# A fused attention-and-MLP kernel: its opening reordered between the queues and engines, its last tile split 512 + 128

## The chip, the cores and the metric

The kernel runs on one core of a Trainium2 chip. The core has five engines with instruction streams of their own: TensorE (PE in the profile; its weight loads are shown as PEld), VectorE (DVE), ScalarE (ACT), GpSimd (POOL) and SyncE (SP), which here only starts transfers and waits. ScalarE starts some transfers too. Each stream is in order: an instruction that waits for a semaphore holds up everything behind it on its engine. The metric is the device time of one execution in microseconds (us), the median of the runs; lower is better.

## The reference, cut to what matters

```
def _layernorm(x): return (x - mean(x)) / sqrt(var(x) + 1e-5)

x  = A_x                      # [1, 2048, 640], bf16
xn = _layernorm(x)
return x + _A_ref(xn, A_wqkv, A_w_phi, A_wo) + _B_ref(xn, B_w1, B_w3, B_w2)

# _A_ref: q, k, v = xn @ wqkv, 32 heads of 20;  pq = q @ w_phi, pk = k @ w_phi
#   phi = [softmax(p), softmax(-p)];  kv = phi_k^T v;  z = sum(phi_k)
#   o = (phi_q @ kv) / (phi_q @ z + 1e-6);  return o @ wo
# _B_ref: (silu(xn @ w1) * (xn @ w3)) @ w2, inner width 1536
```

So the layer norm of the 2048 tokens comes first, and nothing can be multiplied before the first tokens are loaded, normalized and transposed.

## The kernel before

The 2048 tokens are 16 tiles of 128 (tile 0 to 15), each 128 x 640, with tokens on the partitions (x_tok). A projection needs the normalized tile transposed (xnT: features on partitions, five chunks of 128). Tiles 0 to 3 are transposed on TensorE (five transposes each into PSUM, then a copy to xnT); the later ones by transfers.

The kernel is written as a small planner. Each helper (mm, act, tt, dma and so on) records an operation with an engine, the regions that it reads and writes, and a guessed duration; all are issued from one line (L102, transfers L114). Generators (norms, transposes, attention, mlps, outs and others, L729 to L913) yield steps in their own order, and done counts hold one generator back until another has got far enough. The loop at L922 always takes the step that by the guesses can start first; the order in which steps are taken is then fixed as each engine's instruction order, and waits are put in from the recorded regions. So a changed guess or a changed condition can change the order on every engine, while the durations on the chip are what they are.

The opening, which most of the change touches:

- first_loads (L414) issues the loads. SP: tile 0's columns 0 to 319, tile 1, tile 2, the second half of wv (the weights of V, columns 320 to 639), tile 3, the first thirds of w1 and w3, w_phi, and later loads. ScalarE: tile 0's columns 320 to 639, then the first half of wv.
- consts (L434) sets constants; its Exp on a dummy tile is there so that ScalarE's function table is loaded early.
- norms (L729) orders the layer norm of tiles 0 to 3. For tiles 0, 2 and 3 VectorE takes statistics of each half (ln_half, BATCH_NORM_STATS2), joins them (BATCH_NORM_AGGREGATE) and adds eps; GpSimd raises to the power -0.5 (a TENSOR_TENSOR on one column). For tile 1 ScalarE sums the tile and its squares (act_sum), and VectorE (scalar_op, and act_rstd with the eps) and GpSimd finish. ln_apply then normalizes the tile in place, on VectorE for tiles 0 to 3; "apply(t)" below.
- transposes (L791) runs xn_transpose (L515) for tiles 0 to 3 and, after tile 0's, eight dummy matmuls (idle, L510). Tile 0's five transposes are copied in two parts: three chunks by ScalarE, two by VectorE. Tiles 1 to 3 are copied whole by the engine that is free first by the guesses (evac).
- attention (L811) starts with dummy matmuls (warm_up), then multiplies V of tiles 0 to 3 in single steps: five matmuls of 320 columns for the first half of wv, then five for the second; "V0" to "V3" below. v_store writes V from PSUM.
- After that come the first MLP blocks, the fold of w_phi into the key weights, keys, key-value sums, queries, and the output tiles.

The end: out_tile (L696) adds attention and MLP outputs of a tile in PSUM, 17 matmuls over the inner chunks. The last tile (t = 15) does so in two parts, columns 0 to 383 and 384 to 639: 17 matmuls, an add of the residual on VectorE, and a store from SP for each, so that the first part's add and store run beside the second part's matmuls.

Of the kernel before, what the change touches and what calls it, by code (L numbers as in the profile page):

```python
# [43 lines left out]
class _Program:  # L44
# [127 lines left out]
    def commit(self, ops):  # L172
        for o in ops:
            o.idx = len(self.ops)
            o.deps = self.find_deps(o)
            t = self.free[o.eng]
            for d in o.deps:
                t = max(t, d.end + (0.03 if d.eng == o.eng else 0.07))
            o.start = t
            if o.dma:  # L180
                self.free[o.eng] = t + 0.45
                if "T" == o.part:
                    self.free[o.eng] = t + (1.28 if o.cost < 5e5 else o.cost / 105e3)
                self.bus = max(self.bus, t + 0.5) + o.cost / (280e3 if o.part else 305e3)
                if o.part and o.cost > 5e5:
                    self.bus = max(self.bus, self.free[o.eng] + 1.0)
                o.end = self.bus + (1.5 if t < 1 else 1.6 if t < 3.5 or o.part and o.cost < 2e5 else 2.6)
            else:
                o.end = t + o.cost
                self.free[o.eng] = o.end  # L190
            self.ops.append(o)
            if o.eng == "POOL" and not o.dma:
                self.pool = o
            for g in o.reads:
                if isinstance(g, tuple):
# [54 lines left out]
def bass_parallel_sum__linear_kernel_hedgehog__glu_gated_swiglu__prompt_kernel(  # L250
# [11 lines left out]
    bf = DT.bfloat16  # L262
    LAG = 4.0
    QLEAD = 2
    IDLE1, IDLE2 = 11, 8
    f32 = DT.float32
    P = _Program(nc)

# [145 lines left out]
    def first_loads():  # L414
        def half_wv(eng, a):
            P.dma(eng, wv[:, :, a:a + 320], wqkv_t[:, :, 2 * D + a:2 * D + a + 320])

        P.dma("SP", x_tok[:, 0, 0:320], x_t[:, 0, 0:320])
        P.dma("ACT", x_tok[:, 0, 320:D], x_t[:, 0, 320:D])
        load_x(1, 2)  # L420
        load_x(2, 3)
        half_wv("ACT", 0)
        half_wv("SP", 320)
        load_x(3, 4)
        w13(0, 512)
        P.dma("SP", phi_s[:], phi_t)
        P.dma("SP", wqkT[:, DC:2 * DC, :], A_wqkv[:, D:2 * D], True)
        load_x(4, 8)
        load_x(8, 12)
        load_x(12, 16)  # L430
        P.dma("SP", wqkT[:, 0:DC, :], A_wqkv[:, 0:D], True)


    def consts():  # L434
        memset("DVE", t1[:, 2, :], 0.0)
        memset("DVE", warm[:], 0.0)
        act(warm[:], warm[:], ACT.Exp)
        memset("POOL", ident[:], 0.0)
        select(ident[:], 0, [[-1, 128]], 1, ALU.not_equal, 1.0)
        memset("POOL", GM[:], 1.0)  # L440
        select(GM[:], 0, [[128, DC], [-DH, H]], 1, ALU.is_ge, 0.0)
        select(GM[:], DH, [[-128, DC], [DH, H]], -1, ALU.is_gt, 0.0)
        memset("POOL", mhalf[:], -0.5)
# [51 lines left out]

    def ln_apply(t):
        o, m, s, z = x_tok[:, t, :], mv[:, t, 0:1], rstd[:, t, 0:1], rstd[:, t, 1:2]
        if t < 4 or P.free["DVE"] < P.free["ACT"] + 0.45:
            P.op("DVE", "tensor_scalar", [o], [o, m, s],
                 (o, o, m, s, ALU.add if t == 1 else ALU.subtract, ALU.mult),  # L500
                 cost=0.4)
        else:
            P.op("ACT", "activation", [o], [o, s, z], (o, o, ACT.Identity), dict(bias=z, scale=s),
                 cost=0.9)
# [9 lines left out]

    def xn_transpose(t, k):  # L515
        dst = xnT[:, :, t * 128:(t + 1) * 128]
        for j, a, b in ((0, 0, 3), (1, 3, DC)) if t == 0 else ((0, 0, DC),):
            o = PSb[:, (k + j) * 1024:(k + j) * 1024 + 128 * (b - a)].rearrange("p (c n) -> p c n", n=128)
            for dc in range(a, b):
                tr(o[:, dc - a, :], x_tok[:, t, 128 * dc:128 * dc + 128])  # L520
            if t == 0:
                copy(("ACT", "DVE")[j], dst[:, a:b, :], o, 2)
            else:
                evac(dst, o)
# [171 lines left out]
    def out_tile(t, k):  # L696
        b, ti = divmod(t, 4)
        if t + 2 < T:
            load_xres(t + 2)
        chunks = [(oT[:, i, t * 128:(t + 1) * 128], wo_s, i) for i in range(DC)]  # L700
        chunks += [(hT[b][:, i, ti * 128:(ti + 1) * 128], w2_s, i) for i in range(FC)]
        if t == T - 1:
            for q, lo, hi in ((0, 0, 384), (1, 384, D)):
                for n, (l, w, i) in enumerate(chunks):
                    mm(bank(k + q, hi - lo), l, w[:, i, lo:hi], n == 0, n == len(chunks) - 1)
                r = xres[:, t % 4, lo:hi]
                tt("DVE", r, bank(k + q, hi - lo), r, ALU.add)
                finish.append(P.dma("SP", out_t[:, t, lo:hi], r))
            return
        for n, (l, w, i) in enumerate(chunks):  # L710
            for q in range(2):
                mm(bank(k + q, 320), l, w[:, i, 320 * q:320 * q + 320], n == 0, n == len(chunks) - 1)
        r = xres[:, t % 4, :].rearrange("p (b c) -> p b c", c=320)
        tt("DVE", r, bank2(k, 320), r, ALU.add)
        finish.append(P.dma("SP", out_t[:, t, :], xres[:, t % 4, :]))
# [8 lines left out]
                       default=0.0)  # L724
        return min((k for k in range(0, 8, n) if k // 2 not in held), key=free_at)

    done = dict.fromkeys(("w", "ln", "t", "f", "k", "n", "kv", "v", "u", "qp", "qn", "qd", "q", "o", "h"), 0)

    def norms():  # L729
        yield lambda: (first_loads(), consts())  # L730
# [3 lines left out]
        yield lambda: act_sum(1, ACT.Square, mv[:, 1, 1:2], mv[:, 1, 0:1])  # L734
        yield lambda: ln_apply(0)
        done["ln"] = 1
        yield lambda: act_rstd(1)
        yield lambda: ln_half(2, 0)
        while done["t"] < 1:
            yield None  # L740
        yield lambda: ln_apply(1)
        done["ln"] = 2
        yield lambda: ln_half(2, 1)
        yield lambda: ln_rstd(2, 1)
        yield lambda: ln_half(3, 0)
        yield lambda: ln_apply(2)
        done["ln"] = 3
# [37 lines left out]
    def transposed(t):  # L785
        while done["ln"] <= t:
            yield None
        yield lambda: xn_transpose(t, banks(1 if t else 2))
        done["t"] = t + 1

    def transposes():  # L791
        for t in range(4):
            yield from transposed(t)
            if t == 0:
                yield lambda: idle(IDLE2, 128)
# [15 lines left out]
    def attention():  # L811
# [4 lines left out]
        for t in range(4):  # L816
# [4 lines left out]
            for q in range(2):  # L821
                for i in range(DC):
                    yield lambda t=t, q=q, i=i, k=k: v_part(t, q, i, k)
            yield lambda t=t, k=k: v_store(t, k)
            held.clear()
        while done["f"] < 1:
# [194 lines left out]
```

## Time and profile before

| | us |
|---|---|
| median of 3 runs | 269.75 (269.71 to 269.94) |
| the profiled execution's own time | 269.72 |
| its span, first to last instruction | 268.0 |
| TensorE busy | 263.9 (98% of the span) |
| VectorE busy | 171.0 (64%) |
| GpSimd busy | 102.9 (38%) |
| ScalarE busy | 99.5 (37%) |

Times in the profile count from the start of the span; 1.72 us of the profiled execution's time lie outside it. A timeline line reads: start, length, engine, line, operation, output and input tiles, shape, count of merged instructions, and in brackets the idle time before it with what ended it. Matmuls are pipelined: the printed end of one lies behind the start of the next, so rates are taken from starts. "SPq" and "ACTq" are the transfers that SyncE and ScalarE start. Small tiles share names: t is the dummy tile and scratch t1, PS is PSUM, x_tok a token tile, bst and mv statistics, rstd the factor 1/sqrt(var + eps).

### The profile page before, as it was taken

What the parts mean: (1) busy time and instruction counts of PE and PEld (TensorE: products, weight loads), DVE (VectorE), ACT (ScalarE), POOL (GpSimd) and SP (SyncE); (2) the same over time, 40 slices, a digit from 0 to 9 for tenths busy, and PEclk for the clock granted to TensorE, in tenths of its full rate; (3) what the DMA queues carried; (4) which work ended last, traced back from release to release, by engine and by line L of the source; (5) the groups of instructions that cost most, each with busy time, mean ns of one, the idle gap of its engine ahead of it and who ended that gap; (6) DMA issues with size and microseconds to landing.
All of it is one profiled execution on the core that took longest, in us unless ns stands there. A gap on an engine that the chain in (4) does not pass through costs nothing.

```text
span 268.0 us, 4821 instructions
## 1 busy us (share of the span) xinstructions
PE 263.9 (98%) x1962; PEld 161.2 (60%) x1962; DVE 171.0 (64%) x292; ACT 99.5 (37%) x193; POOL 102.9 (38%) x143
## 2 busy tenths in 40 slices
PE   8999999999999999999999999999999999999996
PEld 4656677776745545555555455544577777777774
DVE  4559899998886878888888887888512121212112
ACT  5557979988324443344442344322100000000000
POOL 3316748999995364444444444420000000000000
PEclk9999999999999999999999999999999999999999
DMA  7997695900093444554444444214212213131301
GB/s 217 288 322 152 137 230 109 314 6 2 3 331 67 78 78 81 100 100 93 78 91 92 78 82 78 43 39 78 49 51 73 75 53 97 51 98 49 93 31 49
DMA packets 63510, 27.73 MB, mean 103 GB/s; under 512 B 49792, under 2 KB 63488, under 8 KB 63488
## 3 DMA queue, kind: packets, MB, share of 16 engines
q1 hardware_dynamic: 62688, 26.94, 41.9%
q10 hardware_dynamic: 800, 0.49, 0.7%
q8 instruction: 15, 0.25, 0.4%
q14 instruction: 7, 0.06, 0.1%
HBM read 12.81 MB, written 2.62 MB: 58 GB/s over the span
## 4 chain that ended last, share of the span: by engine, by line
PE 96%; DMA 1%; ACT 1%; DVE 0%; POOL 0%; issue 0%; SPq 0%
PE PS L102 96%; DMA x_tok<-in_A_x_dram 1%; ACT t L102 1%; POOL rstd L102 0%; DVE x_tok L102 0%; DVE xres L102 0%; SPq L114 0%; DVE rstd L102 0%; DVE mv L102 0%
## 5 line engine op out<-in xcount | busy, mean ns | idle before, releaser
L102 PE MATMUL PS<-xnT,w_s 128*128 128x512 bf16 x480 | 107.5, 379 | 0.0
L102 PEld LDWEIGHTS PS<-xnT,w_s 128*128 128x128 bf16 x480 | 45.8, 98 | 51.3 <-ACT Wkp L102 0.2
L102 PE MATMUL PS<-w_s,hT 128*128 128x320 bf16 (+2 forms) x384 | 54.9, 299 | 0.0
L102 DVE TENSOR_TENSOR xres<-PS,xres 128x640 bf16<-128x640 f32 (+2 forms) x17 | 13.4, 785 | 60.0 <-PE PS L102 60.0
L102 ACT ACTIVATE th<-PS 128x512 f32<-128x512 f32 x48 | 28.8, 600 | 49.1 <-PE PS L102 49.1
L102 PEld LDWEIGHTS PS<-w_s,hT 128*128 128x128 bf16 x384 | 37.6, 98 | 14.6
L102 DVE SCALAR_TENSOR_TENSOR t<-th,PS 128x512 bf16<-128x512 f32 x48 | 32.4, 675 | 21.2 <-ACT th L102 21.2
L102 POOL TENSOR_TENSOR ekt<-ekt,rS 128x640 bf16<-128x640 bf16 x32 | 39.5, 1265 | 0.6 <-DVE rS L102 0.6
L102 ACT ACTIVATE eq<-PS 128x600 bf16<-128x600 f32 (+1 forms) x72 | 24.7, 411 | 29.7 <-PE PS L102 29.6
L102 DVE SCALAR_TENSOR_TENSOR hT<-t,PS 128x512 bf16<-128x512 bf16 x48 | 33.0, 687 | 1.7
L102 PE MATMUL PS<-wv,xnT 128*128 128x320 bf16 x160 | 24.7, 299 | 0.1
L102 PE MATMUL PS<-wo_s,oT 128*128 128x320 bf16 (+2 forms) x160 | 24.5, 299 | 0.0
L102 PE MATMUL PS<-Wqp,xnT 128*128 128x512 bf16 (+1 forms) x160 | 24.1, 299 | 0.0
L102 PE MATMUL PS<-Wkp,xnT 128*128 128x320 bf16 x160 | 23.9, 299 | 0.0
L102 ACT ACTIVATE ekt<-PS 128x640 bf16<-128x640 f32 x32 | 22.3, 703 | 3.8 <-PE PS L102 3.3
L102 POOL TENSOR_TENSOR eq<-eq,rq 128x600 bf16<-128x600 bf16 (+1 forms) x32 | 22.6, 728 | 1.3
L102 DVE TENSOR_REDUCE S<-ekt 128x64 f32<-128x1280 bf16 x16 | 23.0, 1438 | 0.0
L102 POOL TENSOR_TENSOR rq<-rq,Sq 128x32 f32<-128x32 f32 x16 | 4.0, 252 | 48.8 <-DVE rq L102 48.8
L102 POOL TENSOR_TENSOR half<-eq 128x660 f32<-128x660 bf16 x15 | 20.4, 1358 | 3.6 <-ACT eq L102 3.6
L102 PEld LDWEIGHTS PS<-wo_s,oT 128*128 128x128 bf16 x160 | 15.7, 98 | 6.3
L102 PEld LDWEIGHTS PS<-wv,xnT 128*128 128x128 bf16 x160 | 15.3, 98 | 6.5 <-ACT xnT L102 0.5
L102 PEld LDWEIGHTS PS<-Wqp,xnT 128*128 128x128 bf16 x160 | 12.8, 97 | 10.5
(55 smaller groups left out, 182.9 us busy)
## 6 DMA issues: line engine op xcount, KB each, us to landing
w_s<-in_B_w_dram SPq DMA_DIRECT2D x6, 640.0 KB, 6.2
xres<-in_A_x_dram SPq DMA_DIRECT2D x16, 160.0 KB, 2.4
out_dram<-xres SPq DMA_DIRECT2D x15, 160.0 KB, 1.8
x_tok<-in_A_x_dram SPq DMA_DIRECT2D x3, 640.0 KB, 6.4
w_s<-in_B_w_dram SPq DMA_DIRECT2D x1, 1920.0 KB, 8.0
wo_s<-in_A_wo_dram SPq DMA_DIRECT2D x1, 800.0 KB, 8.2
x_tok<-in_A_x_dram SPq DMA_DIRECT2D x3, 160.0 KB, 3.9
wv<-in_A_wqkv_dram ACTq DMA_DIRECT2D x1, 400.0 KB, 4.4
```

Source lines behind the costliest of these rows:

```text
L102: o = _Op(eng, lambda: m(*args, **kw), r, w, cost)
```

## The change

Every edit is in the opening or in the last output tile, but for the planner's guesses, from which the whole order is made.

- The load of tile 2 moves from SP to ScalarE's queue, behind the dummy Exp (which moves ahead of it, with its memsets). The first half of wv moves from ScalarE to SP, into the place where tile 2's load was.
- Tile 2 is normalized by GpSimd (tensor_scalar, 128 x 640) instead of VectorE.
- In norms, tile 2's first statistics come before tile 1's eps, and its second before apply(1); tile 3's first statistics wait until tile 1's transposes are placed.
- Tile 1's transposes are placed only after five V matmuls of tile 0 (the count v0).
- The transposes of tiles 1 and 2 are copied in two parts by ScalarE and VectorE, as tile 0's were.
- Five dummy matmuls instead of eight after tile 0's transposes.
- The last tile is split into columns 0 to 511 and 512 to 639; the second part's store is started by ScalarE.
- The planner's guess of when a transfer lands changes for transfers not started by SP.

```diff
-                self.bus = max(self.bus, t + 0.5) + o.cost / (280e3 if o.part else 305e3)
+                self.bus = max(self.bus, t + 0.5 if o.eng == "SP" else 0.0) + o.cost / (280e3 if o.part else 305e3)
...
+                o.end = max(o.end, t + 2.2)
...
-    IDLE1, IDLE2 = 11, 8
+    IDLE1, IDLE2 = 11, 5
...
+        memset("DVE", t1[:, 2, :], 0.0)
+        memset("DVE", warm[:], 0.0)
         P.dma("SP", x_tok[:, 0, 0:320], x_t[:, 0, 0:320])
         P.dma("ACT", x_tok[:, 0, 320:D], x_t[:, 0, 320:D])
         load_x(1, 2)
-        load_x(2, 3)
-        half_wv("ACT", 0)
+        P.op("ACT", "activation", [warm[:]], [warm[:]], (warm[:], warm[:], ACT.Exp), {}, cost=1.4)
+        P.dma("ACT", x_tok[:, 2, :], x_t[:, 2, :])
+        half_wv("SP", 0)
         half_wv("SP", 320)
         load_x(3, 4)
...
     def consts():
-        memset("DVE", t1[:, 2, :], 0.0)
-        memset("DVE", warm[:], 0.0)
-        act(warm[:], warm[:], ACT.Exp)
...
-        if t < 4 or P.free["DVE"] < P.free["ACT"] + 0.45:
+        if t == 2:
+            P.op("POOL", "tensor_scalar", [o], [o, m, s], (o, o, m, s, ALU.subtract, ALU.mult), cost=0.9)
+        elif t < 4 or P.free["DVE"] < P.free["ACT"] + 0.45:
...
-        for j, a, b in ((0, 0, 3), (1, 3, DC)) if t == 0 else ((0, 0, DC),):
+        for j, a, b in ((0, 0, 3), (1, 3, DC)) if t < 3 else ((0, 0, DC),):
...
-            if t == 0:
+            if t < 3:
                 copy(("ACT", "DVE")[j], dst[:, a:b, :], o, 2)
...
-            for q, lo, hi in ((0, 0, 384), (1, 384, D)):
+            for q, lo, hi in ((0, 0, 512), (1, 512, D)):
...
-                finish.append(P.dma("SP", out_t[:, t, lo:hi], r))
+                finish.append(P.dma(("SP", "ACT")[q], out_t[:, t, lo:hi], r))
...
         done["ln"] = 1
+        yield lambda: ln_half(2, 0)
         yield lambda: act_rstd(1)
-        yield lambda: ln_half(2, 0)
         while done["t"] < 1:
             yield None
+        yield lambda: ln_half(2, 1)
         yield lambda: ln_apply(1)
         done["ln"] = 2
-        yield lambda: ln_half(2, 1)
         yield lambda: ln_rstd(2, 1)
+        while done["t"] < 2:
+            yield None
         yield lambda: ln_half(3, 0)
         yield lambda: ln_apply(2)
...
-        yield lambda: xn_transpose(t, banks(1 if t else 2))
+        yield lambda: xn_transpose(t, banks(1 if t > 2 else 2))
...
         for t in range(4):
+            while t == 1 and done["v0"] < DC:
+                yield None
             yield from transposed(t)
...
                     yield lambda t=t, q=q, i=i, k=k: v_part(t, q, i, k)
+                    done["v0"] += 1
```

More of the change, by code (lines that the diff above doesn't have):

```diff
@@ L725, in banks @@
         return min((k for k in range(0, 8, n) if k // 2 not in held), key=free_at)
-    done = dict.fromkeys(("w", "ln", "t", "f", "k", "n", "kv", "v", "u", "qp", "qn", "qd", "q", "o", "h"), 0)
+    done = dict.fromkeys(("w", "ln", "t", "f", "k", "n", "kv", "v", "u", "qp", "qn", "qd", "q", "o", "h", "v0"), 0)
     def norms():
```

## The prediction, made before the changed kernel was run

> **What bounds the kernel now.** I read the span first, then the chain of waits, then the timeline of the opening and of the last tile, then the landings of the first loads.
>
> ```profile
> span 268.0 us, 4821 instructions
> 6.02 0.17 DVE rstd L102
> ...
> 6.85 0.46 DVE x_tok L102
> 7.35 5.00 PE PS L102 x43
> ...
> 19.95 245.56 PE PS L102 x1826
> ```
>
> These pieces of the chain read start, length, what. From 7.35 us it is TensorE to the end of the last matmul; the part from 19.95 on is one unbroken piece of 1826. Work of the middle cannot be hidden better, it can only start earlier. So the edits can gain in two places only: gaps of TensorE before about 14 us, and what follows the last matmul. Ahead of 7.35 stands tile 1's normalization: from its eps instruction (6.02) to its transposes it is 1.33 us.
>
> ```profile
> 6.66 0.45 PE L102 MATMUL PS<-wv,xnT 128*128 128x320 bf16 x2
> 7.35 0.45 PE L102 MATMUL PS<-ident,x_tok 128*128 128x128 bf16 x5 [0.25 <-DVE x_tok L102]
> 7.64 1.79 PE L102 MATMUL PS<-wv,xnT 128*128 128x320 bf16 x12
> 9.29 0.45 PE L102 MATMUL PS<-ident,x_tok 128*128 128x128 bf16 x5
> 10.54 0.66 PEld L102 LDWEIGHTS PS<-wv,xnT 128*128 128x128 bf16 x6 [0.31 <-ACT xnT L102]
> 12.39 1.20 PEld L102 LDWEIGHTS PS<-wv,xnT 128*128 128x128 bf16 x10 [0.38 <-DVE xnT L102]
> 13.77 0.59 PE L102 MATMUL PS<-xnT,w_s 128*128 128x512 bf16 x2
> ```
>
> Printed ends overlap the next start, so I take rates from starts: twelve V matmuls from 7.64 to 9.29, 0.137 us each; five transposes from 7.35 to 7.64, 0.058 each. V of tiles 0 to 3 plus the transposes of tiles 1 to 3 need 40 x 0.137 + 15 x 0.058 = 6.35 us, but lie between 6.66 and 13.77, which is 7.11. So 0.76 us of gaps is all that reordering can win here: about 0.42 before 7.35 (6.66 + 2 x 0.137 = 6.93), the rest mainly where V2 waits at 10.54 for ScalarE's copy and V3 at 12.39 for VectorE's.
>
> **The change, part by part.** *Start of tile 0.* Its loads, statistics and transposes keep their order, so V0 still starts at 6.66: the 0.49 us copy below starts at 6.11. The three dummy matmuls left out lie in that wait: nothing, unless TensorE's clock fell in a longer wait; after the old gap of 0.42 us its rate was the full one above.
>
> ```profile
> 6.09 0.48 DVE L102 BATCH_NORM_STATS2 bst<-x_tok 128x6 f32<-128x320 bf16 x1
> 6.11 0.49 ACT L102 ACTIVATE xnT<-PS 128x384 bf16<-128x384 bf16 x1
> 6.49 0.27 DVE L102 COPY xnT<-PS 128x256 bf16<-128x256 bf16 x1
> 7.21 0.49 DVE L102 BATCH_NORM_STATS2 bst<-x_tok 128x6 f32<-128x320 bf16 x1
> 7.73 0.21 DVE L102 BATCH_NORM_AGGREGATE mv<-bst 128x2 f32<-128x12 f32 x1
> 7.84 0.70 ACT L102 ACTIVATE xnT<-PS 128x640 bf16<-128x640 bf16 x1 [1.24 <-PE PS L102]
> 8.15 0.49 DVE L102 BATCH_NORM_STATS2 bst<-x_tok 128x6 f32<-128x320 bf16 x1
> 8.21 0.55 POOL L102 TENSOR_TENSOR rstd<-rstd,mhalf 128x1 f32<-128x1 f32 x1 [1.39 <-DVE rstd L102]
> 9.15 0.49 DVE L102 BATCH_NORM_STATS2 bst<-x_tok 128x6 f32<-128x320 bf16 x1
> ```
>
> *Loads.* Tile 2's load leaves SP's third place; the first half of wv takes it. On ScalarE's queue the load stands behind the table load and the Exp:
>
> ```profile
> 0.79 1.34 SPq L114 DMA_DIRECT2D x_tok<-in_A_x_dram  x3
> 1.22 0.46 ACTq L114 DMA_DIRECT2D wv<-in_A_wqkv_dram  x1
> 1.71 1.28 ACT L102 ACT_TABLE_LOAD   x1 [1.71 <-PEq L1006]
> 2.17 0.43 SPq L114 DMA_DIRECT2D wv<-in_A_wqkv_dram  x1
> 3.01 0.21 ACT L102 ACTIVATE warm<-warm 128x8 f32<-128x8 f32 x1
> ```
>
> It is issued at about 1.22 + 1.28 + 0.21 + 0.05 = 2.76, a microsecond later than before (third of the three SP issues, about 1.70). When it lands decides the case. Landings, from DMA views of short windows (last number: us from issue), and the queues' traffic from 3.6 to 4.0 us:
>
> ```profile
> x_tok<-in_A_x_dram SPq DMA_DIRECT2D x1, 160.0 KB, 2.8
> wv<-in_A_wqkv_dram ACTq DMA_DIRECT2D x1, 400.0 KB, 4.4
> x_tok<-in_A_x_dram SPq DMA_DIRECT2D x1, 160.0 KB, 3.9
> wv<-in_A_wqkv_dram SPq DMA_DIRECT2D x1, 400.0 KB, 5.5
> ...
> q10 hardware_dynamic: 201, 0.13, 106.9%
> q1 hardware_dynamic: 3, 0.00, 1.1%
> ```
>
> Tile 1 landed at 1.24 + 2.8 = 4.0, the first wv half (ScalarE, q10) at 1.22 + 4.4 = 5.6, tile 2 (SP, q1) at 1.70 + 3.9 = 5.6, the second wv half at 2.17 + 5.5 = 7.65. While tile 2's load stood on q1, q10 moved 201 packets and q1 three: it got through only as the wv half ended. In the new order that half follows tile 1 on SP and still ends in front; if tile 2 then goes ahead of the second half, the same bytes have moved by the same time and it lands by about 5.6 again. I take 5.6; the other bound is 8.1 (a rival). The Trainium skill, page "DMA: Bandwidth & Descriptors", section "Queues, rings and completion order", says that a DMA engine takes turns between the queues' rings packet by packet. By that rule the load waits for one packet and 5.6 is an upper bound; 201 against 3 shows that the turns were not fine ones.
>
> *Tile 1.* VectorE's first statistics of tile 2 now stand ahead of tile 1's eps. They start at 5.6, as tile 2 lands; the eps follows 0.4 later, at 6.0, as before, since neighbours overlap by 0.08 (6.09 + 0.48 against 6.49). ScalarE's sums of tile 1 start earlier, because its load no longer shares with wv, but the eps is held by VectorE's order: no gain. While GpSimd raises to the power, VectorE copies (0.27) and does tile 2's second statistics (0.48), so apply(1) starts at 6.85 to 6.95 and the transposes at 7.35 to 7.45. Now the gap ahead of them holds five V matmuls instead of two: 6.66 + 5 x 0.137 = 7.34. After the transposes (7.64) come five V matmuls instead of eight; they need the second wv half, 7.65, so V0 ends at 8.38 where it was 7.64 + 8 x 0.137 = 8.74: 0.36 gained.
>
> *Tile 2.* Its second statistics no longer stand behind apply(1), so the aggregate comes at 7.21 instead of 7.73 and the power at 7.69 instead of 8.21, ending 8.24. GpSimd's apply follows at 8.30. Its price has no row:
>
> ```profile
> L102 POOL TENSOR_TENSOR ekt<-ekt,rS 128x640 bf16<-128x640 bf16 x32 | 39.5, 1265 | 0.6 <-DVE rS L102 0.6
> L102 POOL MEMSET GM<- 128x160 bf16 x1 | 0.2, 231 | 0.0
> ```
>
> It is below the two-input 1.27 us and not below VectorE's own 0.46 (6.85 in the chain). Four times the 160-column memset is 0.92; I take 0.95. The transposes are ready at 9.30, against 9.29 before. The Trainium skill, "GPSIMD Engine Reference", section "Engine selection", calls one-input work there roughly line-rate, an estimate of 640 / 1.2 GHz (the clock in its table) = 0.53 us plus dispatch; by that the sum would not change, since V1 covers it. V1 runs 8.38 to 10.02 with these five transposes inside. The copies are shared: ScalarE takes 0.49 instead of 0.70 and waits for three transposes instead of five (2 x 0.058), so V2 follows the transposes by 10.54 - 9.29 - 0.32 = 0.93 and starts at 10.23. That is 0.31 gained (at 1.27 us for the apply V2 starts at 10.55: nothing gained here).
>
> *Tile 3.* Its first statistics started at 8.15 and its second at 9.15, with VectorE's apply(2) between them. Now the second follow at 8.15 + 0.41 = 8.56, so everything behind them, to the transposes, is 0.59 earlier and falls into V2, and V3 does not wait as it did at 12.39. V2 ends at 10.23 + 1.37 + 0.29 = 11.89, the single copy (up to 0.70) is done by then, and V3 ends at 13.26 instead of 13.77. The opening gains **0.51 us**.
>
> *Last tile.* 34 matmuls over the same columns: by the 128- and 320-column rates time is linear in columns, so TensorE loses nothing.
>
> ```profile
> 263.68 0.56 DVE L102 TENSOR_TENSOR xres<-PS,xres 128x384 bf16<-128x384 f32 x1 [1.94 <-PE PS L102]
> 265.54 0.42 DVE L102 TENSOR_TENSOR xres<-PS,xres 128x256 bf16<-128x256 f32 x1 [1.30 <-PE PS L102]
> ...
> out_dram<-xres SPq DMA_DIRECT2D x1, 96.0 KB, 1.6
> ...
> out_dram<-xres SPq DMA_DIRECT2D x1, 64.0 KB, 1.5
> ```
>
> The add shrinks by 0.14 per 128 columns: 0.28 for 128, 0.70 for 512. The 512 add runs in the 17 x 0.058 = 0.99 us of the last part. The last store is half as long, but moves rows of 256 bytes and is issued by ScalarE: I put 1.5 again; the two rows, 0.1 apart for 32 KB, give 1.4 below, and 0.2 more than the nearest row, for the queue that no row shows storing, gives 1.7 above. The tail gains 0.14 (from 0.24 to a loss of 0.06).
>
> **Sum.** The profiled execution took 269.72 (0.03 below the median of 269.75): 269.72 - 0.51 - 0.14 = 269.07, call it **269.1**.
>
> **Rivals.**
> 1. *Slower: the loads are served in order of issue across both queues.* Tile 2 then follows both wv halves and lands about where tile 3's load, next to it in the issue order, landed before: 2.65 + 5.5 = 8.1.
>
> ```profile
> 2.65 0.52 SPq L114 DMA_DIRECT2D x_tok<-in_A_x_dram  x1
> x_tok<-in_A_x_dram SPq DMA_DIRECT2D x1, 160.0 KB, 5.5
> ```
>
> VectorE stands at its first statistics; behind them on that engine wait tile 1's eps, the copy that V0's fourth matmul reads, and apply(1). All shift by 8.1 - 5.6 = 2.5, so 271.6. For it: 201 packets against 3. Against: at 4.0 only the wv half, issued before tile 2, was in flight, and all of it may have counted as one turn. It decides from a landing at about 6.25, where the 0.65 gained is gone.
> 2. *Half the gain.* GpSimd's apply takes 1.27, or tile 2 lands near 6.0: V2 starts where it did, 0.2 around V3 and the tail remain: 269.72 - 0.2 - 0.14 = 269.4. For it: no row has this operation on GpSimd. Against: V1 leaves 0.4 us between the transposes' place and its end.
> 3. *The gain does not reach the end*, or the planner's new order differs: times after 14 us are fixed by loads, or it puts V0's second half ahead of tile 1's transposes and TensorE stands for the 7.65 landing. The tail alone remains: 269.72 - 0.14 = 269.6. Against: nothing after 19.95 waits now.
>
> **How the numbers follow.** Forecast 0.60, rival 1 0.16, rival 2 0.15, rival 3 0.09. The forecast's own range is 268.7 (all 0.76 and 0.24) to 269.3 (V0's 0.36 and 0.06); to leave out no more than 2 in 10 the range goes to 269.9, with most of rival 1 outside. No change means within 0.2%, about 0.54 us, which is what a measurement of this kernel can tell: 269.21 to 270.29. Faster: 0.56 of the forecast and 0.02 of rival 2, 0.58. Same: 0.04 + 0.13 + 0.08 = 0.25. Slower: 0.16 + 0.01 = 0.17.
>
> **What would show it.** In the new timeline: five V matmuls from 6.66, transposes at 7.35 to 7.45, V1 from about 8.4, V2 about 10.2, first 512-column matmul at 13.2 to 13.3; GpSimd's 640-column instruction near 8.3 with 0.9 us. VectorE idle before tile 2's first statistics, released by the x_tok load, would be rival 1. The last add should last 0.28. I am wrong if the chain of waits still shows VectorE, GpSimd or a load after 7.4, or if TensorE's unbroken piece begins much earlier and the span is the same.

## The result, and the profile after

| | before | after |
|---|---|---|
| median of 6 runs each, us | 269.76 (269.56 to 269.94) | 270.85 (270.58 to 271.40) |
| ratio to before, with its 95% interval | 1 | 1.0045 (1.0035 to 1.0055) |
| the profiled execution's own time and span | 269.72, 268.0 | 270.58, 268.8 |
| GpSimd busy | 102.9 | 105.4 |

The change makes the kernel slower by 0.45%, some 1.1 us. The forecast was 269.1, and 270.85 lies above the whole range (268.7 to 269.9). The profiled execution is the fastest of the six, so its trace shows 0.86 of the 1.1. The page of the changed kernel begins:

```profile
span 268.8 us, 4797 instructions
```

Its chain of waits (start, length, what) has, where before TensorE's unbroken work began at 7.35:

```profile
7.62 0.56 POOL rstd L102
...
8.28 2.54 POOL x_tok L102
...
11.79 3.17 PE PS L102 x25
```

GpSimd's one instruction on tile 2 holds the chain until 10.87. The timeline of the same kernel shows it together with a second, earlier wait:

```profile
6.63 0.85 PE L102 MATMUL PS<-wv,xnT 128*128 128x320 bf16 x5 [0.19 <-ACT xnT L102]
8.13 0.31 PE L102 MATMUL PS<-wv,xnT 128*128 128x320 bf16 x1 [0.65 <-DMA wv<-in_A_wqkv_dram]
8.28 0.44 PE L102 MATMUL PS<-ident,x_tok 128*128 128x128 bf16 x5
8.28 2.53 POOL L102 TENSOR_SCALAR x_tok<-x_tok,mv,rstd 128x640 bf16<-128x640 bf16 x1
9.75 0.57 PE L102 MATMUL PS<-wv,xnT 128*128 128x320 bf16 x3
10.87 0.45 PE L102 MATMUL PS<-ident,x_tok 128*128 128x128 bf16 x5 [0.55 <-POOL x_tok L102]
15.01 1.24 PE L102 MATMUL PS<-xnT,w_s 128*128 128x512 bf16 x5
```

First, the planner put not five but six V matmuls ahead of tile 1's transposes, and the sixth reads the second half of wv. TensorE stood from about 6.63 + 5 x 0.137 = 7.32 to 8.13 for that load, with tile 1's transposes, whose input VectorE had finished at about 7.25, queued behind it. Second, GpSimd's instruction took 2.53 us, so tile 2's transposes, ready to go at 9.75 + 3 x 0.137 = 10.16, started at 10.87. These two waits are 0.81 + 0.71 = 1.5 us, where V and the transposes had 0.76 us of gaps in all before. The first 512-column matmul is printed at 15.01 (before 13.77). Some records of matmuls are missing in this trace, so I trust the last add's start more: 266.56 against 265.54, 1.02 later.

The loads' issues, again from the timeline:

```profile
1.23 1.28 ACT L102 ACT_TABLE_LOAD   x1 [1.23 <-PEq L1014]
1.30 0.39 ACTq L114 DMA_DIRECT2D x_tok<-in_A_x_dram  x1
2.52 0.21 ACT L102 ACTIVATE warm<-warm 128x8 f32<-128x8 f32 x1
```

Their landings, from DMA views of short windows (last number: us from issue to landing), tile 1, tile 2 and the two halves of wv:

```profile
x_tok<-in_A_x_dram SPq DMA_DIRECT2D x1, 160.0 KB, 2.6
x_tok<-in_A_x_dram ACTq DMA_DIRECT2D x1, 160.0 KB, 2.8
...
wv<-in_A_wqkv_dram SPq DMA_DIRECT2D x1, 400.0 KB, 4.4
...
wv<-in_A_wqkv_dram SPq DMA_DIRECT2D x1, 400.0 KB, 5.9
```

Tile 2's load is behind the Exp in ScalarE's stream, but it was issued at 1.30, while the table load ran and 1.2 us before the Exp. It landed at 1.30 + 2.8 = 4.1, beside tile 1 (3.9); the halves of wv, issued at 1.71 and 2.18, came at 6.1 and 8.1. The tail, from the timeline:

```profile
266.56 0.29 DVE L102 TENSOR_TENSOR xres<-PS,xres 128x128 bf16<-128x128 f32 x1 [0.26 <-PE PS L102]
266.88 0.35 ACTq L114 DMA_DIRECT2D out_dram<-xres  x1
```

and the last store's landing, from the DMA view:

```profile
out_dram<-xres ACTq DMA_DIRECT2D x1, 32.0 KB, 1.5
```

From the last add's start to the end of the span it is 268.8 - 266.56 = 2.24, before 268.0 - 265.54 = 2.46: 0.22 gained. With 1.02 lost ahead of it that is the span's 0.8. The chain has GpSimd at 8.28, which is the prediction's own sign of being wrong (VectorE, GpSimd or a load after 7.4).

### The profile page after: what moved, and what is told of

The parts are those of the page before. It is cut to its first block, busy times and chain, and to the rows that moved or that the text cites. A ratio compares the mean times of both kernels' runs of the same rounds, so it can differ in the third digit from the quotient of the medians.

```text
span 268.8 us, 4797 instructions
## 1 busy us (share of the span) xinstructions
PE 261.7 (97%) x1939; PEld 159.8 (59%) x1959; DVE 170.9 (64%) x293; ACT 99.0 (37%) x193; POOL 105.4 (39%) x144
## 4 chain that ended last, share of the span: by engine, by line
PE 95%; POOL 1%; DVE 1%; DMA 1%; issue 1%; ACT 0%
PE PS L102 95%; POOL x_tok L102 1%; DMA x_tok<-in_A_x_dram 1%; DVE bst L102 1%; POOL rstd L102 0%; DVE x_tok L102 0%; ACT xnT L102 0%; DVE mv L102 0%; DVE rstd L102 0%; DVE xres L102 0%; DVE xnT L102 0%
## 5 line engine op out<-in xcount | busy, mean ns | idle before, releaser
L102 PE MATMUL PS<-xnT,w_s 128*128 128x512 bf16 x464 | 105.7, 379 | 1.0 <-ACT Wkp L102 0.2
L102 PE MATMUL PS<-Wqp,xnT 128*128 128x128 bf16 (+1 forms) x157 | 23.5, 297 | 0.2
L102 PEld LDWEIGHTS PS<-Wkp,xnT 128*128 128x128 bf16 x160 | 15.5, 98 | 6.0
```

What stands on the lines that cost most here:

```text
L102: o = _Op(eng, lambda: m(*args, **kw), r, w, cost)
```

## The experiments

Medians stand beside the runs of the kernel before on the same chip (269.62 to 269.75 in the different groups); ratios are to those.

### Each wait taken away alone, and both

Tile 2 normalized by VectorE again, everything else as changed:

```diff
-        if t == 2:
-            P.op("POOL", "tensor_scalar", [o], [o, m, s], (o, o, m, s, ALU.subtract, ALU.mult), cost=0.9)
-        elif t < 4 or P.free["DVE"] < P.free["ACT"] + 0.45:
+        if t < 4 or P.free["DVE"] < P.free["ACT"] + 0.45:
```

> The changed kernel with tile 2 normalized by VectorE again; nothing else is edited. Theory A (the loss is GpSimd's normalization, 2.53 us where 0.95 was expected): tile 2's transposes come at about 9.9 instead of 10.87, the first MLP matmul at 14.1 to 14.2 instead of 15.01, the time falls by about 0.85 to 270.0. Theory B (the loss is the later landing of the second wv half and TensorE standing for it at 7.3 to 8.1, with one V matmul of tile 0 in front of tile 1's transposes): that wait stays whole, and the time falls by 0.3 at most, 270.55 or more.

V0's second half held behind tile 1's transposes, with GpSimd's apply left in (a second condition keeps the later fold of w_phi where it was):

```diff
     def fold_k():
+        while done["v0"] < 8 * DC:
+            yield None
...
             for q in range(2):
+                while t == 0 and q == 1 and done["t"] < 2:
+                    yield None
                 for i in range(DC):
```

> The changed kernel with V's second half of tile 0 held until tile 1's transposes are placed (and the fold of w_phi held until V is placed, so that its order stays). Theory A: tile 1's transposes move from 8.28 to about 7.35, but tile 2's still wait for GpSimd until 10.86, so the time stays within 0.15 of the changed kernel's 270.85. Theory B: about 0.65 is gained, 270.2.

Both edits:

> Both edits: tile 2 normalized by VectorE, and V's second half of tile 0 behind tile 1's transposes. If the two waits are in series, each hidden by the other, as theory A has it: the first MLP matmul at about 13.8, 269.65, more than the two single gains together. If the waits are independent, the gain is the sum of the two single ones.

| kernel | median us | ratio (95%) |
|---|---|---|
| changed | 270.85 (270.58 to 271.40) | 1.0045 (1.0035 to 1.0055) |
| apply on VectorE | 270.03 (269.47 to 271.72) | 1.0019 (1.0003 to 1.0035) |
| V0's second half behind | 270.76 (270.75 to 271.25) | 1.0044 (1.0032 to 1.0056) |
| both | 269.59 (269.27 to 270.43) | 0.9998 (0.9989 to 1.0007) |

By the medians the apply alone brings 0.82, the order alone 0.09, and both bring 1.26. The interval of the apply alone is wide (1.0003 to 1.0035), so that the two single gains fall short of the joint one is argued from the traces, not shown by the medians. The two waits stand in a row. Where tile 1's transposes go earlier (7.84) but the apply stays on GpSimd, the time won is only waited for again, as the timeline of the kernel with the order mended shows:

```profile
8.83 2.53 POOL L102 TENSOR_SCALAR x_tok<-x_tok,mv,rstd 128x640 bf16<-128x640 bf16 x1
11.41 0.45 PE L102 MATMUL PS<-ident,x_tok 128*128 128x128 bf16 x5 [1.62 <-POOL x_tok L102]
```

The wait for GpSimd is now 1.62 instead of 0.55. Half of that difference is this execution, the slowest of its five (271.25): tile 1 landed 0.6 later, and GpSimd started at 8.83 instead of 8.28. The other half is TensorE's, which came to the wait 0.5 earlier and gained nothing by it.

What the order costs depends on when wv's second half lands. With the apply on VectorE the planner again put six V matmuls first, and the profiled execution (269.57) shows the sixth start as the half landed, at 2.18 + 5.5 = 7.7 instead of 8.1:

```profile
6.72 1.30 PE L102 MATMUL PS<-wv,xnT 128*128 128x320 bf16 x6 [0.24 <-ACT xnT L102]
...
7.86 0.44 PE L102 MATMUL PS<-ident,x_tok 128*128 128x128 bf16 x5
...
13.78 1.46 PE L102 MATMUL PS<-xnT,w_s 128*128 128x512 bf16 x6
```

It is as fast as both edits together. Five of the twelve runs of this kernel lie between 269.47 and 269.64, the others between 269.94 and 271.72; the 0.82 and the order's share are differences of medians over such executions. With both edits tile 2's transposes start at 9.42 and the first 512-column matmul at 13.77, both within 0.2 of before (9.29 and 13.77):

```profile
9.42 0.45 PE L102 MATMUL PS<-ident,x_tok 128*128 128x128 bf16 x5
...
13.77 1.46 PE L102 MATMUL PS<-xnT,w_s 128*128 128x512 bf16 x6
```

### The tail alone

The kernel before with only the last tile's split and the store from ScalarE:

```diff
-            for q, lo, hi in ((0, 0, 384), (1, 384, D)):
+            for q, lo, hi in ((0, 0, 512), (1, 512, D)):
...
-                finish.append(P.dma("SP", out_t[:, t, lo:hi], r))
+                finish.append(P.dma(("SP", "ACT")[q], out_t[:, t, lo:hi], r))
```

> The kernel before with only the last tile's split 512 + 128 and the second store started by ScalarE. The prediction's term is a gain of 0.14 (from 0.24 to a loss of 0.06); the changed kernel's profile shows 2.44 us from TensorE's last matmul to the end of the span where it was 2.67. So 269.5 to 269.6, against a rival under which the later of two stores on two queues costs as much as the shorter add gains: 269.75.

Measured 269.52 (269.32 to 269.72), ratio 0.9992 (0.9984 to 1.0001). The median falls by 0.23 against the before of its group (269.75), as the two traces say (0.22); the interval just reaches 1.

### What GpSimd's apply costs by itself

Two kernels add GpSimd instructions on a scratch tile of their own, at a place where nothing else needs GpSimd, to price the operation; their times say nothing. The first varies the width and the operands of (x - m) * s (the helper's arguments are the columns, m, s and how often; a number stands for a column of them):

```diff
+        ts(640, m, s, 3)
+        ts(640, 0.5, 0.5, 3)
+        ts(320, m, s, 2)
+        ts(160, m, s, 2)
+        ts(640, m, 0.5, 2)
...
+        ts(640, m, s, 2)
```

> The kernel before with GpSimd instructions added beside the output tiles, on a tile of zeros that nothing else uses; its time says nothing. They price GpSimd's tensor_scalar in bf16, subtract and multiply: with two per-partition columns on 640, 320 and 160 columns, with one, with two immediates, and with VectorE taking statistics beside it. Theory A1 (the price is the instruction's own): 2.5 us on 640 columns with VectorE idle and with VectorE busy, in proportion to the columns. Theory A2 (in the opening it shared something with VectorE): 0.9 to 1.3 with VectorE idle, 2.5 only beside it. If the per-partition columns are what costs, the form with immediates is under 1.3.

Groups of instructions, GpSimd's, of that kernel (the numbers behind the bar: busy us, mean ns of one):

```profile
L102 POOL TENSOR_SCALAR probe<-probe,mv,rstd 128x640 bf16<-128x640 bf16 x5 | 12.5, 2504 | 64.8 <-DVE probe L102 64.5
L102 POOL TENSOR_SCALAR probe<-probe 128x640 bf16<-128x640 bf16 x3 | 7.0, 2349 | 0.3
...
L102 POOL TENSOR_SCALAR probe<-probe,mv,rstd 128x160 bf16<-128x160 bf16 x2 | 1.8, 898 | 0.2
```

2.50 us is the price seen in the opening (2.53). Three of the five ran with VectorE idle and the last two beside its statistics, at 2.48 and 2.49, so it is not VectorE's work that slows the instruction. It grows by (2504 - 898) / 480 = 3.3 ns a column over a fixed part of 898 - 160 x 3.3 = 0.37 us, and numbers in place of columns save only 0.15. The second kernel varies the operations:

```diff
+        go("tensor_scalar", (o, o, m, s, ALU.subtract, ALU.mult), [m, s])
+        go("tensor_scalar", (), [], dict(out=o, in0=o, scalar1=0.5, scalar2=None, op0=ALU.add))
+        go("tensor_scalar", (), [s], dict(out=o, in0=o, scalar1=s, scalar2=None, op0=ALU.mult))
+        go("tensor_scalar", (o, o, s, m, ALU.mult, ALU.add), [m, s])
+        go("tensor_tensor", (o, o, s.to_broadcast([128, D]), ALU.mult), [s])
...
```

> The kernel before with further GpSimd instructions beside the output tiles, 640 columns in bf16 on a tile of zeros that nothing else uses; its time says nothing. tensor_scalar with two columns again (2.5 us), with one operation only (an immediate, a column), with multiply then add, and tensor_tensor with a column spread over the width and with the tile itself. If each arithmetic step is a pass of its own, one operation takes about half, 1.2 to 1.4 us; if the form is slow as such, it stays near 2.3. tensor_tensor: 1.2 to 1.3 as in the kernel.

```profile
L102 POOL TENSOR_SCALAR probe<-probe,mv,rstd 128x640 bf16<-128x640 bf16 x2 | 5.0, 2512 | 64.0 <-DVE probe L102 63.9
L102 POOL TENSOR_SCALAR probe<-probe,rstd 128x640 bf16<-128x640 bf16 x2 | 3.8, 1880 | 0.2
L102 POOL TENSOR_SCALAR probe<-probe 128x640 bf16<-128x640 bf16 x2 | 3.6, 1821 | 0.2
L102 POOL TENSOR_TENSOR probe<-probe,rstd 128x640 bf16<-128x640 bf16 x2 | 2.5, 1252 | 0.2
L102 POOL TENSOR_SCALAR probe<-probe,rstd,mv 128x640 bf16<-128x640 bf16 x2 | 1.7, 869 | 0.2
```

Neither expected outcome came (half the price for one operation, or the same price for every form). The price hangs on the operations: subtract then multiply 2.51, one operation alone 1.82 or 1.88, multiply then add 0.87 with the same two columns. This pair costs less than one operation alone and 2.9 times less than subtract then multiply. Whether it is the order or the kind of the operations that sets the price is not shown: multiply then subtract and add then multiply were not tried. The 0.95 that I had put down would have been near for a pair that the change does not use. The Trainium skill, "GPSIMD Engine Reference", section "Engine selection", calls one-input work on GpSimd roughly line-rate. The rows from 0.87 to 2.51 us for the same 640 columns, against 0.45 on VectorE, do not bear that out; the measured rows decide.

### The cheap pair in its place

Tile 2 normalized by GpSimd as x * r + z with z = -m * r, in the changed kernel. The guesses of the added operations are set so that the order of V and the transposes of tiles 1 and 2 stays:

```diff
-            P.op("POOL", "tensor_scalar", [o], [o, m, s], (o, o, m, s, ALU.subtract, ALU.mult), cost=0.9)
+            P.op("POOL", "tensor_scalar", [o], [o, s, z], (o, o, s, z, ALU.mult, ALU.add), cost=0.9)
...
+        if t0 == 2:
+            P.op("DVE", "tensor_scalar", [z], [m], (),
+                 dict(out=z, in0=m, scalar1=-1.0, scalar2=None, op0=ALU.mult), cost=-0.1)
+            P.op("POOL", "tensor_tensor", [z], [z, r], (z, z, r, ALU.mult), cost=-0.1)
```

> The changed kernel, with GpSimd's apply of tile 2 written as x*r + z, z = -m*r (multiply, then add) in place of (x - m)*r. z costs two 128x1 operations, one on VectorE beside rstd's power and one on GpSimd behind it. Theory A (the price of the pair subtract, multiply on GpSimd is what made the change a loss; as measured by itself the pair multiply, add takes 0.87 us): rstd is there at about 8.2, z 0.3 to 0.55 later, the apply ends at about 9.5 to 9.8, before TensorE has done the 11 V matmuls that the order puts ahead of tile 2's transposes (about 10.0). So the wait of 0.88 for GpSimd's x_tok disappears, and the time is that of the kernel with this apply on VectorE, 270.0 (269.7 to 270.3). Rival B: beside VectorE's work, or as one step between two engines, the apply costs the same in any form: no change against the changed kernel, 270.6 to 270.9.

Measured 270.56 (270.24 to 271.49), ratio 1.0032 (1.002 to 1.0043): the time named by the theory (270.0) was missed. Against the changed kernel it is 0.29 less by the medians, but the two intervals overlap, so a gain is not shown. Three of the seven runs (270.24 to 270.26) lie in the theory's range of 269.7 to 270.3. The profiled execution is that of 271.49, the slowest. Its timeline:

```profile
6.30 0.71 PE L102 MATMUL PS<-ident,x_tok 128*128 128x128 bf16 x5 [0.71 <-DVE x_tok L102]
7.38 1.78 PE L102 MATMUL PS<-wv,xnT 128*128 128x320 bf16 x6
8.95 0.74 PE L102 MATMUL PS<-ident,x_tok 128*128 128x128 bf16 x5
9.65 0.87 POOL L102 TENSOR_SCALAR x_tok<-x_tok,rstd 128x640 bf16<-128x640 bf16 x1
10.81 0.57 PE L102 MATMUL PS<-wv,xnT 128*128 128x320 bf16 x3
11.22 0.44 PE L102 MATMUL PS<-ident,x_tok 128*128 128x128 bf16 x5
```

and one row of its table of windows (window, length, then busy time of TensorE, its weight loads, VectorE, ScalarE and GpSimd, the granted clock, DMA):

```profile
8.00:9.00 1.00, 1.00 (x6) 0.54 (x5) 0.42 (x3) 0.00 (x0) 0.47 (x1) 1.00 1.10 349
```

GpSimd's apply takes 0.87 here too, beside VectorE's statistics, and TensorE does not wait for it: the transposes at 11.22 follow three V matmuls from 10.81 without a gap. TensorE was itself late here, though (in the changed kernel's profile it came to this place at 10.16, and the apply above ends at 9.65 + 0.87 = 10.52), so this execution does not show that the wait is gone in a faster one. Two other things stand out in it. Tile 1's load landed late in this execution (1.24 + 3.6 = 4.8), and behind it, on VectorE, stood tile 0's apply, so tile 0's transposes began at 6.30 instead of 5.71 in the changed kernel's profile. And TensorE ran at half its rate for longer: six V matmuls from 7.38 to 8.95 are 0.26 us each, not 0.137, though the window shows a granted clock of 1.00. The Trainium skill, "TensorE: Matmul & The Clock Gate", section "Part 1: The HAM clock gate", has matmuls at 1.2 GHz until a window of about 3.4 us was busy; by that clock 320 columns are an estimated 0.267 us. The trace agrees with that size; it does not test when the rate should rise. Besides, the planner gave tile 3's copy to ScalarE (0.70 instead of VectorE's 0.49). How much each adds to the median was not separated.

The same pair in the best kernel found (below), where VectorE had tile 2:

> The best version so far (V0's second half behind tile 1's transposes, loads as before, copies of tiles 0 to 3 shared, the new tail), with tile 2's apply on GpSimd as multiply, add instead of on VectorE. Theory A: the apply (0.87) and z hide behind the nine V matmuls ahead of tile 2's transposes (tile 2's rstd is there at 8.45, so the apply would end near 9.8, 0.65 after the 9.15 at which VectorE's let the transposes start; the order moves V matmuls in between), VectorE is free 0.43 earlier for tile 3's statistics, whose wait of 0.20 ahead of its transposes goes: 269.0 to 269.2. Rival B: the two extra steps and the hop cost more than the 0.43 brings: 269.5 or more.

Measured 270.01 (269.84 to 270.37), ratio 1.0009 (1.0000 to 1.0018), against 269.21 with VectorE: the rival's outcome. Timeline:

```profile
7.83 0.55 POOL L102 TENSOR_TENSOR rstd<-rstd,mhalf 128x1 f32<-128x1 f32 x1 [0.86 <-DVE rstd L102]
8.42 0.15 DVE L102 TENSOR_SCALAR rstd<-mv 128x1 f32<-128x1 f32 x1 [0.66 <-POOL rstd L102]
8.65 0.19 POOL L102 TENSOR_TENSOR rstd<-rstd 128x1 f32<-128x1 f32 x1 [0.27 <-DVE rstd L102]
8.96 0.88 POOL L102 TENSOR_SCALAR x_tok<-x_tok,rstd 128x640 bf16<-128x640 bf16 x1
9.89 0.45 PE L102 MATMUL PS<-ident,x_tok 128*128 128x128 bf16 x5 [0.71 <-POOL x_tok L102]
```

I had VectorE's part of z beside the power. It waits for it (z lies in the same small tile as rstd, and the program made it wait): from the power's end at 8.38 to the apply at 8.96 it is 0.58 us of steps of 0.15 and 0.19 and the hops between engines. The transposes start at 9.89, 0.73 later than with VectorE (9.16), and the time is 0.80 longer. There is no slack here: with VectorE (the best version's profile), nine V matmuls from 7.86 end at 7.86 + 9 x 0.137 = 9.09, and the apply ends at 8.67 + 0.43 = 9.10.

### The loads

Both mends with the loads as before:

```diff
-        P.op("ACT", "activation", [warm[:]], [warm[:]], (warm[:], warm[:], ACT.Exp), {}, cost=1.4)
-        P.dma("ACT", x_tok[:, 2, :], x_t[:, 2, :])
-        half_wv("SP", 0)
+        load_x(2, 3)
+        half_wv("ACT", 0)
+        P.op("ACT", "activation", [warm[:]], [warm[:]], (warm[:], warm[:], ACT.Exp), {}, cost=1.4)
```

> As e3_both (tile 2 normalized by VectorE, V's second half of tile 0 behind tile 1's transposes), and the loads as in the kernel before: tile 2 third on SyncE's queue, the first wv half on ScalarE's. Every compute engine has the same order as in e3_both. Theory C (the new order of loads costs time of its own: tile 1 lands later because tile 2 is issued beside it at 1.30 and not at 2.76): tile 1's eps comes at about 6.0 instead of 6.2, its transposes at 7.35, the first MLP matmul at 13.4 to 13.5 instead of 13.77, 269.25 and a narrower spread of the runs. Rival: the loads' order does not matter once GpSimd and the order are mended, 269.6 as e3_both.

The other way round, the kernel before with the new loads alone:

```diff
-        load_x(2, 3)
-        half_wv("ACT", 0)
+        P.dma("ACT", x_tok[:, 2, :], x_t[:, 2, :])
+        half_wv("SP", 0)
```

> The kernel before with the new order of loads alone (tile 2 on ScalarE's queue, both wv halves on SyncE's); no compute engine's order changes. Theory C: tile 1 lands 0.1 to 0.4 later, its transposes with it, 269.85 to 270.15, and the runs spread wider than the 0.4 of the kernel before. Rival: no difference, 269.75.

All loads but tile 0's second half in one line on SP (tile 1, first half of wv, tile 2, second half, tile 3), with both mends and all copies of tiles 0 to 3 shared:

```diff
-        P.dma("ACT", x_tok[:, 2, :], x_t[:, 2, :])
         half_wv("SP", 0)
+        load_x(2, 3)
         half_wv("SP", 320)
```

> As e9_four_shared, but the loads in one line on SyncE's queue: tile 1, first wv half, tile 2, second wv half, tile 3; ScalarE's queue has only its half of tile 0. No compute engine's order changes. Theory D (tile 1 sharing the transfer engines with the first wv half is what makes it land at 4.0): it lands at about 3.5 to 3.7, but VectorE takes tile 2's statistics ahead of tile 1's eps and tile 2 still lands at about 5.6, so the time stays at 269.2, within 0.15. Rival: an earlier tile 1 is worth 0.3, 268.9; or one queue alone feeds the transfer engines less well and all later loads slip by 0.3 to 0.4, as in e7_loads_only, 269.5 or more.

| kernel | median us | ratio (95%) |
|---|---|---|
| both mends, new loads | 269.59 (269.27 to 270.43) | 0.9998 (0.9989 to 1.0007) |
| both mends, loads as before | 269.31 (269.08 to 269.56) | 0.9984 (0.9975 to 0.9993) |
| before, new loads alone | 270.21 (269.74 to 270.30) | 1.0009 (0.9999 to 1.0019) |
| all in line on SP | 269.94 (269.60 to 270.77) | 1.0007 (0.9993 to 1.0020) |

The new loads cost 0.28 by the medians (0.38 by the ratios; the two ran on different chips) in the one pair, and in the other between 0.24 (by the ratio) and 0.5 (by the medians, 270.21 against 269.70). The intervals alone would not part them from nothing, but both pairs and the traces point the same way. From issue to landing tile 1 took 2.6 to 3.6 us in the seven traces with the new loads and 2.6 to 2.9 in the eight with the loads as before; wv's first half 4.2 to 5.9 (issued at 1.71) and 3.7 to 4.6 (issued at 1.22); its second half, issued at 2.18 in both, 5.4 to 6.9 and 5.1 to 5.6. In the kernel before with the new loads, the DMA view has tile 2 and tile 1:

```profile
x_tok<-in_A_x_dram ACTq DMA_DIRECT2D x1, 160.0 KB, 3.4
x_tok<-in_A_x_dram SPq DMA_DIRECT2D x1, 160.0 KB, 3.1
```

and the timeline:

```profile
7.07 0.43 PE L102 MATMUL PS<-wv,xnT 128*128 128x320 bf16 x2 [0.26 <-DMA wv<-in_A_wqkv_dram]
7.76 0.45 PE L102 MATMUL PS<-ident,x_tok 128*128 128x128 bf16 x5 [0.26 <-DVE x_tok L102]
```

Two tiles that are in flight on two queues at once land together (1.25 + 3.1 = 4.4 and 1.22 + 3.4 = 4.6), and V0 waits for wv until 7.07 where it started at 6.66. That they share is what the rule of turns in the Trainium skill, "DMA: Bandwidth & Descriptors", section "Queues, rings and completion order", would have; nothing here tells how fine the turns are. In one line on SP, tile 1 landed after 2.3, with nothing on the second queue but tile 0's half, as theory D had it. But the 269.2 that it named was missed: tile 2 came too late instead, and VectorE stood for it ahead of tile 1's eps, as that kernel's timeline shows:

```profile
6.53 0.49 DVE L102 BATCH_NORM_STATS2 bst<-x_tok 128x6 f32<-128x320 bf16 x1 [0.83 <-DMA x_tok<-in_A_x_dram]
...
8.25 0.45 PE L102 MATMUL PS<-ident,x_tok 128*128 128x128 bf16 x5 [0.48 <-DVE x_tok L102]
```

That is the mechanism of my first rival, at a smaller price: tile 2's statistics at 6.53 instead of 5.60 and tile 1's transposes at 8.25 instead of 7.57 in the best version below, which has the same orders and the loads as before; the median is 0.73 longer. It did not happen in the changed kernel.

### The best version

Both mends, the loads as before, the new tail, and tile 3's copy shared by ScalarE and VectorE too:

```diff
-        for j, a, b in ((0, 0, 3), (1, 3, DC)) if t < 3 else ((0, 0, DC),):
+        for j, a, b in ((0, 0, 3), (1, 3, DC)) if t < 4 else ((0, 0, DC),):
...
-            if t < 3:
+            if t < 4:
...
-        yield lambda: xn_transpose(t, banks(1 if t > 2 else 2))
+        yield lambda: xn_transpose(t, banks(2))
```

> As e5_old_loads, and tile 3's copy shared by ScalarE and VectorE too; otherwise the same orders. V3's wait for VectorE's whole copy (0.2 in e3_both) falls to under 0.05: 0.15 faster than e5_old_loads, about 269.1. If the wait is only put off to the next instruction, no difference.

Measured 269.21 (268.97 to 269.81), ratio 0.9977 (0.9968 to 0.9987): faster than both kernels. The step from 269.31, which is tile 3's copy alone, is within the noise. Its timeline:

```profile
9.16 0.45 PE L102 MATMUL PS<-ident,x_tok 128*128 128x128 bf16 x5
...
11.40 2.17 PE L102 MATMUL PS<-wv,xnT 128*128 128x320 bf16 x14
13.62 1.67 PE L102 MATMUL PS<-xnT,w_s 128*128 128x512 bf16 x7
```

Fourteen V matmuls from 11.40 need 1.92 and end at about 13.32: no wait is left at V3. What lies between that and 13.62 is about one 512-column matmul, whose record may be missing.

### What spreads the runs with the new loads

The kernel with both mends spreads by 1.2 us and that with only the apply mended by 2.3, with the loads as before by 0.5 to 0.8. (The kernel before spreads by 0.5 in most groups, but had single runs of 270.89 and 271.54.) To tell late loads from TensorE's half rate, dummy matmuls fill TensorE's waits around tile 0's transposes; nothing else differs from the kernel with both mends:

```diff
-    IDLE1, IDLE2 = 11, 5
+    IDLE1, IDLE2 = 14, 8
```

> The kernel with both mends (apply of tile 2 on VectorE, V0's second half behind tile 1's transposes) and the new loads, with 14 instead of 11 dummy matmuls of 128 columns before tile 0's transposes and 8 instead of 5 behind them; nothing else differs. In the profile of the multiply-add kernel, TensorE stood for 1.0 us at 5.3 and its matmuls ran at half rate (0.267 us a V matmul) until 10.0, in the others the full rate began between 4.1 and 7.0. Theory C (TensorE's rate is raised only after a stretch in which it was busy, and the waits in the opening put that off in some executions; this makes the spread of the kernels with the new loads): the dummies fill the 0.45 to 0.6 us at 5.3 and the 0.4 ahead of V0, no profile shows half rate after 7, the spread of 269.27 to 270.43 shrinks to about 0.5 us, the median goes from 269.59 to 269.35 to 269.5. Rival: the spread comes from the loads' landings alone: spread and median as they were, 269.5 to 269.7, or up to 0.2 more where the dummies run late and hold the transposes.

The same in the best version:

> The same two counts of dummy matmuls in the best version so far (before's loads, all copies of tiles 0 to 3 shared; 269.21, from 268.97 to 269.81). Theory C: its full rate began at 7.0 in the profile, so some 0.1 to 0.2 us of half-rate V matmuls go: 269.0 to 269.2, with a narrower spread. Rival (loads alone): 269.2, or up to 0.2 more by dummies that hold the transposes.

Measured 269.49 (269.22 to 270.58), against 269.59 (269.27 to 270.43) without the dummies, and 269.22 (268.97 to 269.70) against 269.21. Neither median nor spread moved, so the theory of the half rate found no support. The profiled execution of the first is its slowest, 270.58. The DMA view has the first half of wv, and the timeline what waited for it:

```profile
wv<-in_A_wqkv_dram SPq DMA_DIRECT2D x1, 400.0 KB, 5.9
```

```profile
7.78 0.84 PE L102 MATMUL PS<-wv,xnT 128*128 128x320 bf16 x5 [1.17 <-DMA wv<-in_A_wqkv_dram]
```

It was issued at 1.71 and landed at 7.6, 1.5 later than in the changed kernel's profile (6.1). TensorE stood 1.17 us for it, at full rate afterwards (5 x 0.137 from 7.78 to 8.46). So a late load makes a slow execution without any half rate; whether the half rate adds to some, as it may in the multiply-add kernel's, stays open.

## Why the prediction was wrong

The step that failed is the price of GpSimd's apply in the paragraph on tile 2: "I take 0.95", between 0.46 and 1.27. It took 2.53, twice the upper bound. The bound came from a two-input instruction with one operation, the lower estimate from a memset; neither does the subtract and multiply whose pair sets the price. The guess that the planner was given (cost=0.9 in the diff) was as far off. With 2.53, transposes "ready at 9.30" started at 10.87. Rival 2 had the right place but stopped at 1.27. Taking the apply back to VectorE brought 0.82 by the medians, of the 1.75 us between 269.1 and 270.85.

The second step that failed is tile 1's: "the gap ahead of them holds five V matmuls instead of two". The planner placed six, and TensorE stood for wv, which now landed at 8.1, not 7.65. I had this as half of rival 3, at a chance of 0.09 and with the tail as the only thing left; it does not lose only the gain, it moves tile 1's transposes from 7.35 to 8.28. Once the apply was mended, the order was worth another 0.44 by the medians (270.03 to 269.59), but nothing in the one profiled execution with six V matmuls first and the apply on VectorE (269.57), where the half landed at 7.7.

The third is the loads. The issue at 2.76, behind the Exp, was wrong: 1.30. Tile 2 then landed at 4.1, not 5.6, which did no harm by itself, so rival 1 had no occasion. But with the new loads tile 1 and both halves of wv landed later in most traces, and the median is 0.28 longer (269.59 against 269.31), with a wider spread. That "V0 still starts at 6.66" held in the changed kernel's profile (6.63), but in the seven traces with the new loads it starts between 6.63 and 7.78, in the eight with the loads as before between 6.66 and 6.93.

What held: the tail, 0.14 with up to 0.24 allowed, measured 0.22, its add 0.29 where 0.28 was forecast and its store 1.5 from issue to landing as put down. The gain of the intended order is shown only in part. With VectorE's apply, five V matmuls ahead of tile 1's transposes, and the loads as before, the kernel takes 269.31, and 269.21 with tile 3's copy shared, beside the 269.1 of the sum. Of these gains of 0.39 and 0.49 on their chip the tail has 0.23, which leaves 0.16 and 0.26 for the opening where 0.51 was forecast, and the intervals overlap with that of the tail alone. In the traces the stretch from V0's start to the last add is 258.52 and 258.36 us, against 258.88 in the kernel before and 258.68 in that with the new tail alone: 0.16 to 0.52 shorter. The remaining 0.1 to 0.2 of the sum cannot be assigned to a step.

## What to carry to other kernels

An operation whose price no row shows should be bounded by rows with the same operations on the same engine, or not at all: here the pair of operations moved the price by 2.9 times at equal shape, and the neighbour with the same shape was no bound. Where two waits stand in a row on one engine, mending the earlier one alone shows little (0.09), so a small effect of one edit does not clear it. A wait for a load is worth what the load's landing makes of it: look at the spread of the runs before putting a price on it from one median. In a kernel ordered by guesses, read the new order itself before pricing it: one matmul more ahead of the transposes tied them to a load.

## What the runs showed of the hardware that was not expected

- GpSimd's tensor_scalar on 128 x 640 bf16 took 2.51 us for subtract then multiply, 1.82 to 1.88 for one operation, 0.87 for multiply then add. Why is open; other pairs of operations were not tried.
- A transfer issued from ScalarE's stream was not held by the table load and the Exp ahead of it: issued at 1.30, the Exp started at 2.52.
- A load of 400 KB, issued at 1.70 or 1.71 in every case, landed between 4.2 and 5.9 us later in seven traces with the same order of loads. What delays it is open.
- Two loads of 160 KB on two queues, issued at 1.24 and 1.30, landed within 0.3 us of each other in the changed kernel's profile (3.9 and 4.1); the first took 2.3 where it had no such neighbour.
- In one execution TensorE's matmuls ran at half rate until about 10 us with a granted clock shown as 1.00. What sets the moment of the full rate was not tried beyond the dummies.
